# Two copies out of PSUM in an induced attention, moved to ScalarE in a planned kernel

## The chip, the cores and the metric

The kernel runs on one core of a Trainium2 chip. The metric is device time in microseconds (us), of one launch; the runs of the kernel before are 1744.55, 1745.02 and 1746.68 us, so their median is 1745.02.

## The reference

The input `x` is 4 batches of 12480 tokens with 128 channels. An induced attention with 32 learned points comes first, then a feed-forward layer with a squared relu, for every token:

```
scale = 1.0 / np.sqrt(C)
def mab(q, kv):
    s = scale * (q @ kv.transpose(0, 2, 1))
    s = s - s.max(-1, keepdims=True)
    a = np.exp(s)
    a /= a.sum(-1, keepdims=True) + 1e-09
    return a @ kv
h = mab(I, x)              # 32 rows a batch: the first attention
y = mab(x, h)              # every token on the 32 rows: the second attention
h = np.maximum(y @ w_in, 0.0)      # 128 -> 2048
out = h * h @ w_out                # 2048 -> 128
```

## The kernel before, in words

The tokens of a batch are cut into 13 units of 960; there are 52 units, and a unit has two halves of 480 tokens. Three kinds of work run side by side.

*The first attention* (class `First`) of a unit takes scores (`na` with `indT`, L430), a running maximum (`mx`, `neg`), an exponential (`e`), a transpose (`ep`, copied to `et`) and a product (`nb`) that is added to `hacc` and `zs`. It runs 14 units ahead of the feed-forward layer, so the last 13 or so units of the program have none of it. After the 13 units of a batch `first_end` joins the four partial results and makes `hT` and the matrix `hw`, which is `hT` times `w_in`; this is the change of batch, and the next batch's second attention starts from it.

*The second attention* (class `Second`) of a unit is done while the unit before it is in the feed-forward layer. Its scores `na` (L626) are 128 by 240 numbers in PSUM. `evict` copies them to SBUF as `ss` (L639, through the helper `copy`, so the profile has it at L235); `turn` transposes them on TensorE to `s2t`; `top` and `sub` (VectorE) take the maximum (`mx2`) and the difference `d`; `power` (ScalarE) is the exponential; `total`, `safe`, `invert` and `share` (VectorE) are the sum `z2`, its reciprocal `rz2` and the weights in `d`; `high` and `low` split them into `sk`; `back` turns them on TensorE into `ap`, 128 by 480 in PSUM; `stacked` copies `ap` to `sw` (L696, also L235 in the profile); `spread` sends `sw` with four DMAs on SP to `st`, the tile that the feed-forward layer of the next unit reads.

*The feed-forward layer* (`ffn_block`) does a half in four chunks (`quad`). A chunk has four matmuls `h` of 480 columns on `st` and `hw` into two double-bank PSUM tiles (there are two in all), two relus on ScalarE into `g` (L790), one square in place (L801), then on VectorE the rounded part `hi` (L805) and the rest `lo` (L809), and on TensorE 12 matmuls `op` (L822): `hi` with `wo_hi`, `hi` with `wo_lo`, `lo` with `wo_hi`. After the four chunks VectorE transposes `op` into `rows` (L837) and SP stores them.

The order of all this is not written out: every step is a task with an engine, a cost, a due time and what it needs, and the class `Plan` lays the tasks on the engines before anything is issued. Of the tasks that can start, an engine takes the one that is due first. A task for `"ACT|DVE"` goes to the engine where the plan lets it start first. Each engine then works through its instructions in that order, and an instruction that waits holds up all behind it.

Of the kernel before, what the change touches and what calls it, by code (L numbers as in the profile page):

```python
# [24 lines left out]
BLK = UNIT // 2  # L25
# [19 lines left out]
class Plan:  # L45
# [15 lines left out]
    def add(self, engine, ns, fn, due, needs=(), port=False, mode=None, takes=(), reads=(), late=None):  # L61

        if late is None:
            late = self.LATE["PE" if engine == "PE" else "other"] if due > self.begin else 0.0
        needs = [n for n in needs if n is not None]
        t = Task(engine.split("|"), ns, fn, due, needs, port, mode, takes, late, len(self.tasks))  # L70
        for b in list(takes) + list(reads):
            b.users.append(t)
        self.tasks.append(t)
        return t
# [80 lines left out]
def induced_attention_then_squared_relu_ffn(  # L155
# [8 lines left out]
    nc = tc.nc  # L164
# [10 lines left out]
    PERIOD, START, T_MAIN, NARROW, STEP = 32000.0, 2600.0, 66000.0, 6000.0, 1700.0  # L175
    W_DUE = [8000.0 + 6500.0 * k for k in range(8)]

    ST = "ACT|DVE"
    LATE_G1, LATE_OT = 150.0, 400.0


# [12 lines left out]
    def bank(name):  # L194
        return ps_m.tile([P, 512], F32, tag="m", name=name)
# [35 lines left out]
    add = plan.add  # L231
    ENG = {"ACT": nc.scalar.copy, "DVE": nc.vector.tensor_copy}

    def copy(task, dst, src):
        ENG[task.by](dst, src)  # L235
# [381 lines left out]
    class Second:  # L617
# [14 lines left out]
        def weigh(self, scored, where, bank_, due, step):  # L632
            v = {}
            n, s, u = self.n, self.s, self.u
            G = 2 * Q

            def evict():
                v["ss"] = att.tile([P, 2 * TS], F32, tag="ss", name=f"ss_{n}")
                copy(te, v["ss"], where())  # L639

            def turn():
                v["tp"] = tp = bank(f"s2t_{n}")
                for k in range(2):
                    nc.tensor.transpose(
                        tp[:TS, k * P:(k + 1) * P], v["ss"][:, k * TS:(k + 1) * TS], ident
                    )

            def top():
                v["tv"] = v["tp"][:TS, :2 * P].rearrange("t (g m) -> t g m", m=M)
                v["mx"] = tiny.tile([TS, G, 1], F32, tag="mx2", name=f"mx2_{n}")  # L650
                nc.vector.tensor_reduce(v["mx"], v["tv"], axis=AX.X, op=ALU.max)

            def sub():
                v["d"] = att.tile([TS, G, M], F32, tag="d", name=f"d_{n}")
                nc.vector.tensor_sub(v["d"], v["tv"], v["mx"].broadcast_to([TS, G, M]))

            def power():
                nc.scalar.activation(v["d"], v["d"], AF.Exp, scale=scale)

            def total():  # L660
                v["z"] = tiny.tile([TS, G, 1], F32, tag="z2", name=f"z2_{n}")
                nc.vector.tensor_reduce(v["z"], v["d"], axis=AX.X, op=ALU.add)

            def safe():
                nc.vector.tensor_scalar_add(v["z"], v["z"], 1e-9)

            def invert():
                v["rz"] = tiny.tile([TS, G, 1], F32, tag="rz2", name=f"rz2_{n}")
                nc.vector.reciprocal(v["rz"], v["z"])

            def share():
                nc.vector.tensor_mul(v["d"], v["d"], v["rz"].broadcast_to([TS, G, M]))  # L672

            def high():
                v["sk"] = att.tile([TS, Q, 2, 2, M], F32R, tag="sk", name=f"sk_{n}")
                nc.vector.tensor_copy(v["sk"][:, :, :, 0, :], v["d"].rearrange("t (k q) m -> t q k m", q=Q))

            def low():
                sk = v["sk"]
                nc.vector.tensor_sub(  # L680
                    sk[:, :, :, 1, :], v["d"].rearrange("t (k q) m -> t q k m", q=Q), sk[:, :, :, 0, :]
                )

            def back():
                v["ap"] = ap = bank(f"ap_{n}")
                for q in range(Q):
                    nc.tensor.matmul(  # L687
                        ap[:, q * TS:(q + 1) * TS],
                        v["sk"][:, q].rearrange("t k a m -> t (k a m)"),
                        identr[:TS, :TS], start=(q == 0), stop=(q == Q - 1), skip_group_check=True,  # L690
                    )

            def stacked():

                v["sw"] = att.tile([P, BLK], F32R, tag="sw", name=f"sw_{n}")
                copy(ts, v["sw"], v["ap"][:, :BLK])  # L696

            def spread():
                st = att.tile([P, 2, BLK], F32R, tag="st", name=f"st_{n}")
                for k in range(2):  # L700
                    for j in range(2):
                        nc.sync.dma_start(
                            st[j * 64:(j + 1) * 64, k, :].bitcast(F32),
                            v["sw"][k * 64:(k + 1) * 64, :].bitcast(F32),
                        )
                s["st", u] = st

            bt, ba, bw = Buffer("m"), Buffer("m"), Buffer("sw")
            self.bst = Buffer("st")
            d = due  # L710
            te = add("DVE", 317, evict, d, [scored], reads=[bank_])
            t = add("PE", 150, turn, d + step, [te], takes=[bt])
            t = add("DVE", 340, top, d + step, [t], reads=[bt])
            td = add("DVE", 340, sub, d + step, [t], reads=[bt])
            tp = add("ACT", 307, power, d + 2 * step, [td])
            t = add("DVE", 330, total, d + 3 * step, [tp])
            t = add("DVE", 70, safe, d + 3 * step, [t])
            t = add("DVE", 115, invert, d + 3 * step, [t])
            t = add("DVE", 340, share, d + 4 * step, [t], port=True)
            th = add("DVE", 210, high, d + 4 * step, [t], port=True)  # L720
            tl = add("DVE", 335, low, d + 5 * step, [th], port=True)
            t = add("PE", 460, back, d + 5 * step, [tl], takes=[ba])
            ts = add(ST, (455, 565), stacked, d + 6 * step, [t], takes=[bw], reads=[ba])
            self.ready = add("SP", 1000, spread, d + 7 * step, [ts], takes=[self.bst], reads=[bw])

    def narrow(second, f, g, due, step, begun=None):
# [193 lines left out]
```

## Time and profile before

| | us |
|---|---|
| runs of the kernel | 1744.55, 1745.02, 1746.68 |
| the profiled execution | 1748.76 |
| its span, first to last instruction | 1746.8 |
| TensorE busy (matmuls) | 1687.7 |
| VectorE busy | 1665.2 |
| ScalarE busy | 1588.2 |

In the lines of the profile PE is TensorE, PEld its weight loads, DVE VectorE, ACT ScalarE, SPq the DMA queue of SP. A line of a timeline has the start in us from the span's beginning, the length, the engine, the line of the kernel, the operation, what it writes and reads, how many are merged in it, and in brackets how long its engine sat idle before it and what ended that. A group has a count, the busy time in us, the mean length in ns, and the idle time before it. In the stretches each pair is busy time and number of instructions, in the order TensorE, weight loads, VectorE, ScalarE, GpSimd, then the granted clock, the share of the DMA engines and GB/s. Tile numbers are left out, so `mx` stands for the maxima of both attentions and `d` for all that is done in that tile.

The first 130 us or so are the loading of the weights and the first batch's first attention; then units follow each other in 32 us, and from about 1340 us on, where no first attention is left, in 29 to 31 us.

### The profile page before, as it was taken

To read this page: it belongs to the slowest core of one execution; us is meant where nothing else is said; L and a number is where in the kernel's file an instruction comes from. 1 tells how busy PE (TensorE), PEld (TensorE's weight loads), DVE (VectorE), ACT (ScalarE), POOL (GpSimd) and SP (SyncE) were. 2 spreads that over 40 slices of the span, in tenths; PEclk is the share of its full clock that TensorE was granted. 3 is DMA by queue.
4 is the path that set the end of the run, shared out by engine and by line. 5 is a ranking of instruction groups with operands and counts; after the bars stand their busy time and mean duration, and the time that the engine had idled before them with its cause. 6 is when DMAs were issued, how large, how long until landed. Compare 5 with 4: busy or idle time off the path is not lost.

```text
span 1746.8 us, 23651 instructions
## 1 busy us (share of the span) xinstructions
PE 1687.7 (97%) x8897; PEld 1339.3 (77%) x8897; DVE 1665.2 (95%) x1777; ACT 1588.2 (91%) x1581; POOL 25.8 (1%) x22
## 2 busy tenths in 40 slices
PE   7699999999999999999999999999999999999998
PEld 4378777777877777777777877777787888888886
DVE  5689999999999999999999999999999999999998
ACT  5399999999989999999998999999998999999997
POOL 1200000000000000000000000000000000000000
PEclk9699999999999999999999999999999999999999
DMA  9742342333333333333423333423211121211111
GB/s 207 128 68 47 63 74 53 62 68 63 61 59 57 60 66 63 63 57 63 73 47 63 64 56 63 74 47 62 40 29 35 29 40 29 41 29 37 32 27 30
DMA packets 428781, 101.61 MB, mean 58 GB/s; under 512 B 362844, under 2 KB 428156, under 8 KB 428668
## 3 DMA queue, kind: packets, MB, share of 16 engines
q1 hardware_dynamic: 428668, 100.11, 31.7%
q8 instruction: 70, 1.15, 0.3%
q14 instruction: 43, 0.35, 0.1%
HBM read 48.94 MB, written 25.56 MB: 43 GB/s over the span
## 4 chain that ended last, share of the span: by engine, by line
PE 51%; DVE 30%; issue 11%; ACT 6%; DMA 2%; SPq 0%; DVEq 0%; POOL 0%; ACTq 0%
PE op L822 35%; PE h L782 12%; DVE lo L809 10%; DVE hi L805 10%; ACT g L801 3%; ACT g L790 2%; DVE rows L837 2%; DVE xt L401 1%; PE na L626 1%; DMA xn<-in_x_dram 1%; DVE sw L235 1%; DVE d L672 1%; DVE sk L680 1%; PE wp L586 1%; DMA words_o<-in_moe_w_out_dram 1%
## 5 line engine op out<-in xcount | busy, mean ns | idle before, releaser
L809 DVE TENSOR_TENSOR lo<-g,hi 128x1920 fp32r<-128x1920 f32 x416 | 896.0, 2154 | 16.2 <-PE na L430 0.5
L790 ACT ACTIVATE g<-h 128x960 f32<-128x960 f32 x832 | 783.0, 967 | 96.1 <-PE h L782 82.6
L801 ACT ACTIVATE g<-g 128x1920 f32<-128x1920 f32 x416 | 752.9, 1810 | 8.2
L782 PE MATMUL h<-st,hw 128*128 128x480 f32 x1664 | 517.9, 389 | 12.7 <-ACT g L790 8.2
L805 DVE CAST hi<-g 128x1920 fp32r<-128x1920 f32 x416 | 477.6, 1148 | 25.1 <-ACT g L801 19.7
L822 PE MATMUL op<-lo,wo_hi 128*128 128x480 f32 x1664 | 459.3, 390 | 15.2 <-DVE lo L809 15.1
L822 PE MATMUL op<-hi,wo_hi 128*128 128x480 f32 x1664 | 462.6, 386 | 1.3 <-DVE hi L805 1.0
L822 PE MATMUL op<-hi,wo_lo 128*128 128x480 f32 x1664 | 432.3, 382 | 0.0
L782 PEld LDWEIGHTS h<-st,hw 128*128 128x128 f32 x1664 | 308.7, 189 | 104.3 <-ACT g L790 54.3
L822 PEld LDWEIGHTS op<-lo,wo_hi 128*128 128x128 f32 x1664 | 297.4, 189 | 87.5 <-DVE lo L809 42.0
L822 PEld LDWEIGHTS op<-hi,wo_hi 128*128 128x128 f32 x1664 | 304.1, 188 | 68.7 <-DVE hi L805 20.2
L822 PEld LDWEIGHTS op<-hi,wo_lo 128*128 128x128 f32 x1664 | 313.8, 189 | 49.9
L837 DVE STREAM_TRANSPOSE rows<-op 128x480 f32<-128x480 f32 x104 | 70.4, 677 | 1.3 <-PE op L822 1.2
L401 DVE STREAM_TRANSPOSE xt<-xq 128x960 f32<-128x960 f32 x39 | 45.7, 1172 | 4.3 <-PE na L626 4.3
L687 PEld LDWEIGHTS ap<-identr,sk 120*128 120x128 f32 x208 | 31.4, 193 | 7.3 <-issue 4.0
L626 PE MATMUL na<-xt,hT 128*32 128x240 f32 x416 | 32.7, 387 | 0.0
L687 PE MATMUL ap<-identr,sk 120*128 120x120 f32 x208 | 29.5, 265 | 2.5 <-DVE sk L680 2.5
L235 ACT COPY xt<-xtp 128x480 f32<-128x480 f32 x26 | 14.3, 559 | 16.4 <-PE xtp L415 16.4
L564 POOL TENSOR_SCALAR sums<-ones,zs 128x128 f32<-128x128 f32 x4 | 8.8, 2209 | 1228.1 <-PE lp L548 800.0
L464 PE MATMUL ep<-ident,e 128*120 128x128 f32 x104 | 21.5, 290 | 5.0 <-ACT e L456 3.3
L415 PE MATMUL xtp<-ident,xn 120*128 120x120 f32 x104 | 18.6, 319 | 7.6 <-DMA xn<-in_x_dram 7.6
L430 PE MATMUL na<-xt,indT 128*32 128x240 f32 x312 | 23.8, 378 | 0.9 <-DVE xt L401 0.9
(90 smaller groups left out, 616.6 us busy)
## 6 DMA issues: line engine op xcount, KB each, us to landing
xn<-in_x_dram SPq DMA_DIRECT2D x52, 480.0 KB, 4.9
st<-sw SPq DMA_DIRECT2D x208, 120.0 KB, 2.3
out_dram<-rows SPq DMA_DIRECT2D x416, 60.0 KB, 2.0
xq<-in_x_dram SPq DMA_DIRECT2D x156, 120.0 KB, 3.6
words_i<-in_moe_w_in_dram SPq DMA_DIRECT2D x4, 512.0 KB, 10.2
words_o<-in_moe_w_out_dram SPq DMA_DIRECT2D x4, 512.0 KB, 9.2
ind_sb<-in_inducing_dram SPq DMA_DIRECT2D x1, 16.0 KB, 1.6
```

The source lines that it names most:

```text
L235: ENG[task.by](dst, src)
L401: nc.vector.transpose(self.xt, v["xq"].rearrange("p g c -> p (g c)"))
L430: nc.tensor.matmul(where[q * M:(q + 1) * M, :], indT, self.xt[:, q * 2 * TS:(q + 1) * 2 * TS], start=True, stop=True,)
L626: nc.tensor.matmul(where[q * M:(q + 1) * M, :].rearrange("m (k t) -> m k t", k=2), self.s["hT"][:, :M], self.s["xt"][self.u].rearrange("c ...
L687: nc.tensor.matmul(ap[:, q * TS:(q + 1) * TS], v["sk"][:, q].rearrange("t k a m -> t (k a m)"), identr[:TS, :TS], start=(q == 0), stop=(q ...
L782: nc.tensor.matmul(c["hp"][:, l, :BLK], s["hw"][:, f * P:(f + 1) * P], s["st", u][:, k, :], start=True, stop=True,)
L790: nc.scalar.activation(v["g"][:, 2 * i:2 * i + 2, :], c["hp"][:, :, :BLK], AF.Relu)
L801: nc.scalar.activation(v["g"], v["g"], AF.Square)
L805: nc.vector.tensor_copy(v["hi"], v["g"])
L809: nc.vector.tensor_sub(v["lo"], v["g"], v["hi"])
L822: nc.tensor.matmul(w["op"][:, :BLK], wo[:, 4 * j + l, :], v[name][:, l, :], start=(j == m == l == 0), stop=(j == NQ - 1 and m == 2 and l = ...
L837: nc.vector.transpose(w["rows"].rearrange("p g c -> p (g c)"), w["op"][:, :BLK])
```

## The change

Both copies are made by ScalarE in all units. Before, `ss` was always VectorE's, and `sw` went to the engine that the plan chose: VectorE for 34 units, ScalarE for 18. The costs that the plan reckons with are 300 for `ss` (it was 317 on VectorE) and 437 for `sw` (it was 455 on ScalarE, 565 on VectorE).

```diff
-    ST = "ACT|DVE"
...
             def evict():
                 v["ss"] = att.tile([P, 2 * TS], F32, tag="ss", name=f"ss_{n}")
-                copy(te, v["ss"], where())
+                nc.scalar.copy(v["ss"], where())
...
                 v["sw"] = att.tile([P, BLK], F32R, tag="sw", name=f"sw_{n}")
-                copy(ts, v["sw"], v["ap"][:, :BLK])
+                nc.scalar.copy(v["sw"], v["ap"][:, :BLK])
...
-            te = add("DVE", 317, evict, d, [scored], reads=[bank_])
+            te = add("ACT", 300, evict, d, [scored], reads=[bank_])
...
-            ts = add(ST, (455, 565), stacked, d + 6 * step, [t], takes=[bw], reads=[ba])
+            ts = add("ACT", 437, stacked, d + 6 * step, [t], takes=[bw], reads=[ba])
```

Since the plan is made anew, the order changes on every engine, also among instructions that the diff does not name. Three places matter here. In the names, `hi_1_5_1_2` is the rounded part of batch 1, unit 5, half 1, chunk 2; `h_1_6_0_0` is the first pair of `h` of the next unit; the last number is a count.

VectorE in the second half of unit 5 of batch 1, before:

```order
L680 TENSOR_TENSOR sk_1_6_6562<-d_1_6_6492,sk_1_6_6562 120x8x32
L837 STREAM_TRANSPOSE rows_1_5_0_6583<-op_1_5_0_6411 128x480
L805 CAST hi_1_5_1_1_6593<-g_1_5_1_1_6547 128x1920
L235 CAST sw_1_6_6605<-ap_1_6_6588 128x480
L809 TENSOR_TENSOR lo_1_5_1_1_6611<-g_1_5_1_1_6547,hi_1_5_1_1_6593 128x1920
L805 CAST hi_1_5_1_2_6628<-g_1_5_1_2_6577 128x1920
```

And now:

```order
L675 CAST sk_1_6_6579<-d_1_6_6492 120x8x32
L836 STREAM_TRANSPOSE rows_1_5_0_6582<-op_1_5_0_6411 128x480
L679 TENSOR_TENSOR sk_1_6_6579<-d_1_6_6492,sk_1_6_6579 120x8x32
L804 CAST hi_1_5_1_1_6594<-g_1_5_1_1_6545 128x1920
L808 TENSOR_TENSOR lo_1_5_1_1_6607<-g_1_5_1_1_6545,hi_1_5_1_1_6594 128x1920
L804 CAST hi_1_5_1_2_6627<-g_1_5_1_2_6575 128x1920
```

The `sw` between `hi` and `lo` is gone from VectorE, and both parts of `sk` stand around `rows`.

TensorE at the border from unit 5 to unit 6 of batch 1, before:

```order
L822 MATMUL op_1_5_1_6570<-lo_1_5_1_1_6611,wo_hi_110 128x480 x4
L822 MATMUL op_1_5_1_6570<-hi_1_5_1_2_6628,wo_hi_110 128x480 x4
L782 MATMUL h_1_6_0_0_6641<-st_1_6_6615,hw_1_4611 128x480 x2
L822 MATMUL op_1_5_1_6570<-hi_1_5_1_2_6628,wo_lo_111 128x480 x4
L782 MATMUL h_1_6_0_1_6652<-st_1_6_6615,hw_1_4611 128x480 x2
```

And now:

```order
L821 MATMUL op_1_5_1_6566<-lo_1_5_1_1_6607,wo_hi_110 128x480 x4
L821 MATMUL op_1_5_1_6566<-hi_1_5_1_2_6627,wo_hi_110 128x480 x4
L821 MATMUL op_1_5_1_6566<-hi_1_5_1_2_6627,wo_lo_111 128x480 x4
L781 MATMUL h_1_6_0_0_6645<-st_1_6_6622,hw_1_4608 128x480 x2
L781 MATMUL h_1_6_0_1_6650<-st_1_6_6622,hw_1_4608 128x480 x2
```

All eight matmuls on `hi` of chunk 2 stand ahead of the new unit's first `h`; before, four of them did. At every second border of the middle it is six.

ScalarE at the start of a unit without a first attention (unit 6 of batch 3), before:

```order
L790 ACTIVATE g_3_6_0_0_14178<-h_3_6_0_1_14182 128x960
L801 ACTIVATE g_3_6_0_0_14178<-g_3_6_0_0_14178 128x1920
L790 ACTIVATE g_3_6_0_1_14204<-h_3_6_0_2_14192 128x960
L790 ACTIVATE g_3_6_0_1_14204<-h_3_6_0_3_14206 128x960
L801 ACTIVATE g_3_6_0_1_14204<-g_3_6_0_1_14204 128x1920
L790 ACTIVATE g_3_6_0_2_14239<-h_3_6_0_4_14232 128x960
L790 ACTIVATE g_3_6_0_2_14239<-h_3_6_0_5_14247 128x960
L658 ACTIVATE d_3_7_14250<-d_3_7_14250 120x256
```

And now:

```order
L789 ACTIVATE g_3_6_0_0_14180<-h_3_6_0_1_14178 128x960
L638 COPY ss_3_7_14199<-na_3_7_14183 128x240
L800 ACTIVATE g_3_6_0_0_14180<-g_3_6_0_0_14180 128x1920
L789 ACTIVATE g_3_6_0_1_14211<-h_3_6_0_2_14202 128x960
L789 ACTIVATE g_3_6_0_1_14211<-h_3_6_0_3_14213 128x960
L800 ACTIVATE g_3_6_0_1_14211<-g_3_6_0_1_14211 128x1920
L789 ACTIVATE g_3_6_0_2_14243<-h_3_6_0_4_14228 128x960
L789 ACTIVATE g_3_6_0_2_14243<-h_3_6_0_5_14245 128x960
L657 ACTIVATE d_3_7_14252<-d_3_7_14252 120x256
```

`ss` has come in between a relu and its square. Between the square and the exponential stand two relus, before and now; in every second unit the old order had one of them ahead of the square. On VectorE the sum `z2` stood behind the second `lo` of the unit where two relus came between, and ahead of it in the others; now it stands ahead of it in all.

## The prediction

> **What bounds the kernel now.** I read the busy time by stretches first, then VectorE's timeline through one unit, then the chain of waits in the same stretch. Columns of the first: length, then busy time of TensorE, its weight loads, VectorE and ScalarE, the granted clock, DMA.
>
> ```profile
> 300.00:500.00 200.00, 196.69 (x1041) 156.43 (x1040) 196.85 (x213) 186.24 (x183) 3.12 (x1) 1.00 0.34 61
> ...
> 1500.00:1700.00 200.00, 198.94 (x948) 163.50 (x947) 195.34 (x183) 193.78 (x175) 0.00 (x0) 1.00 0.17 32
> ```
>
> Three engines are nearly full in both regimes. In the long middle VectorE has 3.15 us idle in 200, ScalarE 13.8; in the last stretch, where no first attention is left, ScalarE has 6.2. So work taken from VectorE and given to ScalarE is worth what VectorE's own row of work and the waits between the engines leave of it. VectorE's timeline, one unit from its first `hi` to the next unit's (start, duration):
>
> ```profile
> 606.30 1.16 DVE L805 CAST hi<-g 128x1920 fp32r<-128x1920 f32 x1 [0.21 <-ACT g L801]
> ...
> 609.96 0.40 DVE L235 COPY ss<-na 128x240 f32<-128x240 f32 x1
> 610.27 0.15 DVE L449 SCALAR_TENSOR_TENSOR neg<-mx,neg 128x1 f32<-128x1 f32 x1
> ...
> 627.70 1.12 DVE L805 CAST hi<-g 128x1920 fp32r<-128x1920 f32 x1
> ...
> 629.30 2.14 DVE L809 TENSOR_TENSOR lo<-g,hi 128x1920 fp32r<-128x1920 f32 x1
> 631.36 1.15 DVE L805 CAST hi<-g 128x1920 fp32r<-128x1920 f32 x1
> 632.62 2.16 DVE L809 TENSOR_TENSOR lo<-g,hi 128x1920 fp32r<-128x1920 f32 x1
> 634.70 1.15 DVE L805 CAST hi<-g 128x1920 fp32r<-128x1920 f32 x1
> ...
> 638.33 1.16 DVE L805 CAST hi<-g 128x1920 fp32r<-128x1920 f32 x1 [0.22 <-ACT g L801]
> ```
>
> The unit takes 638.33 - 606.30 = 32.03 us. A `hi` and `lo` take 634.70 - 631.36 = 3.34, so two pairs 6.68; but 631.36 to 638.33 is 6.97. VectorE thus waits 0.29 once a unit, at the unit's first `hi`, and 31.74 is its own. What it waits for is the end of the chain (start, length, work):
>
> ```profile
> 610.68 0.59 DVE rows L837
> ...
> 613.53 0.31 DVE mx L651
> ...
> 615.90 0.33 DVE d L655
> 616.24 1.07 DVE hi L805
> ...
> 629.38 2.07 DVE lo L809
> 631.50 2.21 PE op L822 x8
> 633.71 0.44 PE h L782 x2
> 634.14 0.86 PE op L822 x4
> 635.01 0.45 PE h L782 x2
> 635.48 0.98 ACT g L790
> 636.49 1.82 ACT g L801
> 638.33 1.17 DVE hi L805
> ```
>
> Up to 631 the chain is mostly VectorE (a few of its steps stand at the top); then it leaves for TensorE (products of the old unit, the first two `h` of the new one) and ScalarE (relu, square) and comes back to the new unit's first `hi`.
>
> **The change, part by part.** The groups of the copies (count, busy us, mean ns):
>
> ```profile
> L235 DVE CAST sw<-ap 128x480 fp32r<-128x480 f32 x34 | 22.1, 650 | 0.0
> ...
> L235 DVE COPY ss<-na 128x240 f32<-128x240 f32 x52 | 20.8, 400 | 1.7 <-PE na L626 1.5
> ...
> L235 ACT COPY et<-ep 120x256 f32<-120x256 f32 x52 | 19.4, 374 | 3.7 <-PE ep L464 3.5
> ...
> L235 ACT CAST sw<-ap 128x480 fp32r<-128x480 f32 x18 | 9.9, 548 | 0.9 <-PE ap L687 0.9
> ```
>
> *Copies on ScalarE.* 52 `ss` and 34 `sw` go over; 18 `sw` were there already. `ss` never ran on ScalarE in this trace: its price lies between nothing, where ScalarE would have idled, and the 0.374 of `et`, which is a little longer; `sw` has its own row, 0.548. Together at most 0.92 us a unit, against 13.8 x 32.03/200 = 2.2 us idle in the middle and 6.2 x 29.9/200 = 0.9 in the tail. I take them as hidden in the middle. If that cover is gone, they cost what they last.
> [...]
>
> *VectorE's own time, middle.* `ss` costs the step 610.27 - 609.96 = 0.31. `sw` stands between a `hi` and its `lo`: 629.30 - 627.70 = 1.60 with it, 632.62 - 631.36 = 1.26 without, so only 0.34 comes back, not 0.65. That is 0.65 a unit. The new order also moves `z2` and `sk` in every second unit out of such a gap, where up to 0.2 is free; I take 0.2 off for those, 0.55 on average. VectorE's own way would be about 31.2.
>
> *The wait at the unit's border, middle.* The order shows that TensorE now does eight (every second unit: six) of the old unit's matmuls on its last-but-one `hi` before the first `h` of the new unit, where it did four.
>
> ```profile
> 628.87 0.73 PEld L822 LDWEIGHTS op<-hi,wo_hi 128*128 128x128 f32 x4
> ...
> 630.49 0.19 PEld L782 LDWEIGHTS h<-st,hw 128*128 128x128 f32 x1
> ...
> 633.33 0.40 PEld L782 LDWEIGHTS h<-st,hw 128*128 128x128 f32 x2
> ...
> 634.18 0.97 ACT L790 ACTIVATE g<-h 128x960 f32<-128x960 f32 x1 [0.25 <-PE h L782]
> ...
> 638.21 1.81 ACT L790 ACTIVATE g<-h 128x960 f32<-128x960 f32 x2
> ```
>
> From that `hi` (631.36) its matmuls start 1.21 later (in the chain: 631.50 + half of the eight, 632.57); eight take 630.49 - 628.87 = 1.62; a relu starts 634.18 - 633.33 = 0.85 after its `h`; two relus in a row are 1.81 - 0.97 = 0.84 apart; square follows relu by 636.49 - 635.48 = 1.01, and `hi` follows square by 638.33 - 636.49 = 1.84. With eight ahead: 1.21 + 1.62 + 0.85 + 0.84 + 1.01 + 1.84 = 7.37, a wait of 0.69. With six ahead the second `h` decides, 0.43 after the eight: 1.21 + 1.62 + 0.43 + 0.85 + 1.01 + 1.84 = 6.96, a wait of 0.28 as now. Mean 0.49, 0.20 more than now. Going through both kinds of unit step by step with these durations, TensorE also comes some 0.1 late to that `hi`, because it waits for `h` buffers that relu frees behind the two copies. So 0.25 of the 0.55 is lost: 0.30 a unit is left. Its ends are 0.55 (no added wait) and 0 (0.55 of it). Of the 34 units with both copies on VectorE five lie at a change of batch; 29 x 0.30 = 8.7 us, ends 16 and 0.
> `sw` also feeds the spread, four DMAs on SP, and the first `h` waits for them. On ScalarE `sw` stands behind a square (1.82) and no longer behind a `hi`, and on SP the spread no longer finds the four output stores of the half before ahead of it; the new order asks for `st` four matmuls, 0.86, later. I count nothing; if `st` is late all the same, by up to 1.82 - 0.86 = 0.96, the middle gains nothing and the border rival below holds.
>
> *The change of batch, three times.* There ScalarE starves and the chain runs through `sw`:
>
> ```profile
> 499.01 1.79 ACT L801 ACTIVATE g<-g 128x1920 f32<-128x1920 f32 x1
> ...
> 501.63 0.66 DVE L235 CAST sw<-ap 128x480 fp32r<-128x480 f32 x1
> ...
> 506.77 1.84 ACT L790 ACTIVATE g<-h 128x960 f32<-128x960 f32 x2 [3.26 <-PE h L782]
> ```
>
> On ScalarE `sw` follows this square and ends at 499.01 + 1.79 + 0.55 = 501.35 instead of 502.29: 0.9 earlier, while ScalarE waits 3.26 for the `h` that needs it. Three times 1.0 is 3 us, ends 0 and 5.
>
> *The last 12 units.* Here only `ss` moves. VectorE's first `hi` two units apart, then two small jobs of TensorE:
>
> ```profile
> 1443.10 1.16 DVE L805 CAST hi<-g 128x1920 fp32r<-128x1920 f32 x1
> ...
> 1502.94 1.15 DVE L805 CAST hi<-g 128x1920 fp32r<-128x1920 f32 x1
> ```
>
> ```profile
> 1436.87 0.16 PEld L626 LDWEIGHTS na<-xt,hT 128*32 128x32 f32 x8 [0.34 <-issue]
> ...
> 1437.41 0.30 PEld L782 LDWEIGHTS h<-st,hw 128*128 128x128 f32 x2 [0.39 <-issue]
> ...
> 1441.19 0.36 PEld L644 LDWEIGHTS s2t<-ident,ss 128*120 128x120 f32 x2
> ```
>
> Two units take 59.84, 29.92 each. VectorE saves between nothing (an `ss` that stood in the free time between a `hi` and its `lo`) and 0.31 a unit; I take 0.15. Its waits now come to less than 4.66 x 29.92/200 = 0.70 a unit, since the 0.11 between a `hi` and its `lo` (632.62 - 631.36 - 1.15) is in that idle time; I take 0.35. But the exponential now stands behind both relus of a chunk on ScalarE in every unit, and `z2`, which reads it, stands on VectorE ahead of the second `lo`, with all of VectorE's work queued behind it; the old order had the one or the other in a unit, not both. The chain from the third-last `lo` of the old unit to that `z2`: matmuls on a `lo` start 631.50 - 629.30 = 2.20 after it; the order has 46 matmuls of 480 columns from there to the `h` of the second relu, 46 x 0.86/4 = 9.9; `na` takes 0.54 + 0.34 = 0.88 of TensorE's time, `s2t` 0.36; the relu starts 0.85 after its `h`, the exponential 0.84 after the relu, and lasts some 0.4 (as `et` of its size). Sum 15.4. VectorE's own way between the same points is 2.07 for that `lo`, three pairs 10.02, and `mx2`, `rows`, `d` and a `hi`, 0.31 + 0.59 + 0.33 + 1.07: 14.4. So it waits 1.0 a unit where it waited 0.35: 0.5 lost with the 0.15 counted. Matmuls that come earlier than I reckon would shorten it, so I take 0.45: 12 x 0.45 = +5.4 us. The ends are -1.8 (no wait added, 0.15 saved) and +8 (0.65 lost).
>
> *The opening* has one `ss` to move and its `sw` is on ScalarE already: taken as nothing, ends -0.4 and +0.4, the length of one copy.
>
> Sum: -8.7 - 3 + 5.4 = -6.3 us on the profiled execution, 1748.76 us (span 1746.8): 1742.5. That execution lies 3.7 above the median of the runs, 1745.02; on that scale 1738.7. A measurement of this kernel can tell 0.2%, 3.5 us, from no change.
>
> **The rivals.**
> *VectorE's time comes back whole.* If TensorE reaches the border earlier than I reckon and no wait grows, the middle gives 16, the batch changes 5, the middle gives 16, the batch changes 5, the tail 1.8: 1745 - 23 = 1722. For it speaks VectorE's 98% and a chain that is mostly VectorE; against it the four extra matmuls ahead of `h`. Chance 0.18.
> [...]
> *The border eats it all.* The wait grows by 0.55 and the tail loses its 5.4: -3 + 5.4 = +2, 1747. Chance 0.22.
> *ScalarE becomes the bound (slower).* The copies stand ahead of relus that free the PSUM buffers for the next `h`. If ScalarE's idle time does not lie where they land, a middle unit takes 0.92 more on ScalarE while VectorE's 0.55 is lost in waits: +0.37 x 29 = 10.7, and with the tail's 8 and nothing at the batch changes 1745 + 19 = 1764. It decides from the point where less than 0.92 of ScalarE's 2.2 us idle time lies behind the copies, before the next square is due. Against it: the idle time is spread over waits for `h` all through the unit. Chance 0.08.
> That the change doesn't move the copies is excluded: the order shows all 104 on ScalarE.
>
> **How the numbers follow.** My case has 0.52. Its own time is 1738.7, taken as 1739, and its terms together spread by some 6 us: I put 0.38 of it below 1741.5 (0.2% under the median), 0.12 within 0.2% and 0.02 above. The border case is 0.02 faster, 0.16 within 0.2% and 0.04 slower, the full return faster, the ScalarE case slower. Faster 0.38 + 0.02 + 0.18 = 0.58; same 0.12 + 0.16 = 0.28; slower 0.02 + 0.04 + 0.08 = 0.14. The range goes from a little above the full return, 1725, to the border case with a worse tail, 1749; it leaves out half of the full return and the ScalarE case.
>
> **What would show it.** Right: `ss` near 0.36 and `sw` 0.55 on ScalarE; middle units alternating about 31.6 and 31.9; VectorE's wait at a unit's first `hi` near 0.3 and 0.7; tail units all alike near 30.4, with VectorE idle ahead of `z2`; the batch changes about 1 us shorter. Wrong: middle units of 31.3 or less, or of 32.0 and more; a tail below 29.9; ScalarE with no idle time left.

## The result, and the profile after

| | before | after |
|---|---|---|
| median of 4 runs, us | 1745.42 (1744.55 to 1746.68) | 1733.72 (1732.35 to 1735.98) |
| ratio | | 0.9934, 95% interval 0.9916 to 0.9951 |
| the profiled execution, us | 1748.76 | 1732.54 |

The change makes the kernel 11.7 us faster; 6.3 had been forecast. The two profiled executions differ by 16.2, since the one of before lies 3.3 above its median and the one of after 1.2 below.

First the two groups of the copies in the changed kernel (count, busy us, mean ns, idle time before them):

```profile
L695 ACT CAST sw<-ap 128x480 fp32r<-128x480 f32 x52 | 28.9, 556 | 4.0 <-PE ap L686 3.9
L638 ACT COPY ss<-na 128x240 f32<-128x240 f32 x52 | 18.7, 360 | 5.5 <-DVE mx L442 4.8 <-PE na L625 0.4 <-PE na L429 0.2
```

All 104 are on ScalarE, at 0.36 and 0.56 us. The same two stretches as before the change:

```profile
300.00:500.00 200.00, 198.34 (x1049) 158.23 (x1048) 195.05 (x201) 189.18 (x195) 3.19 (x1) 1.00 0.34 63
1500.00:1700.00 200.00, 197.14 (x939) 161.26 (x939) 192.07 (x170) 195.29 (x180) 0.00 (x0) 1.00 0.19 35
```

VectorE was busy for 196.85 and 195.34 of 200, now for 195.05 and 192.07; ScalarE went from 186.24 and 193.78 to 189.18 and 195.29. VectorE waits more, although the kernel is faster. Where it waits is in its timeline; these are the first `hi` of four successive units of the middle:

```profile
629.98 1.16 DVE L804 CAST hi<-g 128x1920 fp32r<-128x1920 f32 x1 [0.65 <-ACT g L800]
...
661.55 1.16 DVE L804 CAST hi<-g 128x1920 fp32r<-128x1920 f32 x1 [0.21 <-ACT g L800]
...
693.39 1.16 DVE L804 CAST hi<-g 128x1920 fp32r<-128x1920 f32 x1 [0.65 <-ACT g L800]
...
724.71 1.16 DVE L804 CAST hi<-g 128x1920 fp32r<-128x1920 f32 x1 [0.22 <-ACT g L800]
```

A unit's length is the distance between two such rows: 31.84 with the wait of 0.65 at its end, 31.32 with that of 0.22. VectorE's own time is what is left, 31.19 and 31.10. From here on the wait is always the one in the brackets. In the kernel before that is 0.22, and its own time 32.03 - 0.22 = 31.81; the prediction's 0.29 and 31.74 came from the pace of `hi` and `lo`, by which each of these waits comes out about 0.07 longer. (One unit has a further wait: 629.98 to 661.55 is 31.57.) In the last 12 units VectorE waits twice, at the first `hi` and for the exponential, ahead of `z2`:

```profile
1514.16 1.16 DVE L804 CAST hi<-g 128x1920 fp32r<-128x1920 f32 x1 [0.26 <-ACT g L800]
...
1520.22 0.42 DVE L661 TENSOR_REDUCE z<-d 120x8 f32<-120x256 f32 x1 [0.33 <-ACT d L657]
```

From the first `hi` of every unit follow the lengths by part; the experiments below are read by the same table. "Middle" is the mean of 27 units (2 to 10, 15 to 23, 28 to 36, counted from 0), "joins" the sum of the ten around the changes of batch (11 to 14, 24 to 27, 37, 38), "tail" the mean of the last 12 distances (39 to 50).

| kernel | middle | joins | tail |
|---|---|---|---|
| before | 32.03 | 334.9 | 29.93 |
| after | 31.57 | 330.9 | 30.17 |

27 x 0.455 = 12.3 and 3.9 are gained, 12 x 0.24 = 2.9 lost; units 0 and 1 give 0.4. That is 13.7 of the 16.2. The first unit also started 2.1 earlier (at 87.98 instead of 90.11; so the opening lasts some 90 us, not the 130 given further up). In two experiments that open just as the changed kernel does it started at 89.02 and 89.76, so most of this is scatter of the opening.

### The profile page after: what moved, and what is told of

It reads as the page before. It is cut to its first block, busy times and chain, and to the rows that moved or that the text cites. A ratio compares the mean times of both kernels' runs of the same rounds, so it can differ in the third digit from the quotient of the medians.

```text
span 1730.8 us, 23735 instructions
## 1 busy us (share of the span) xinstructions
PE 1676.5 (97%) x8897; PEld 1334.2 (77%) x8897; DVE 1636.3 (95%) x1691; ACT 1607.2 (93%) x1667; POOL 24.9 (1%) x22
## 4 chain that ended last, share of the span: by engine, by line
DVE 36%; PE 30%; issue 15%; ACT 14%; DMA 1%; DVEq 0%; SPq 0%; ACTq 0%
PE op L821 21%; DVE lo L808 14%; DVE hi L804 13%; ACT g L789 8%; PE h L781 7%; ACT g L800 6%; DVE xt L400 2%; DVE rows L836 2%; DVE z L661 1%; DVE mx L650 1%; DVE sk L679 1%; DVE d L654 1%; DVE mx L442 1%; PE na L625 1%; DVE d L671 0%
## 5 line engine op out<-in xcount | busy, mean ns | idle before, releaser
L781 PE MATMUL h<-st,hw 128*128 128x480 f32 x1664 | 513.4, 388 | 13.4 <-ACT g L789 6.4
L695 ACT CAST sw<-ap 128x480 fp32r<-128x480 f32 x52 | 28.9, 556 | 4.0 <-PE ap L686 3.9
L234 ACT COPY xt<-xtp 128x480 f32<-128x480 f32 x26 | 14.4, 557 | 14.5 <-PE xtp L414 14.2
L585 PE MATMUL wp<-w_in_sb,hT 128*128 128x512 f32 x32 | 20.0, 733 | 6.7 <-DVE hw L594 4.7
L661 DVE TENSOR_REDUCE z<-d 120x8 f32<-120x256 f32 x52 | 21.6, 415 | 3.8 <-ACT d L657 3.8
```

The source lines that it names most:

```text
L695: nc.scalar.copy(v["sw"], v["ap"][:, :BLK])
L781: nc.tensor.matmul(c["hp"][:, l, :BLK], s["hw"][:, f * P:(f + 1) * P], s["st", u][:, k, :], start=True, stop=True,)
```

## The experiments

All are timed against the kernel before on the same chip (its medians there: 1744.77, 1746.07, 1746.05 and 1745.69), and every ratio is to that. Edits are shown against the changed kernel, unless the text says against the kernel before. Where an instruction is moved, the plan's list of tasks is taken as it is and that task is put elsewhere in it; the loop over the units and the conditions are left out there ("...").

**Either half of the change.** With only `sw` always on ScalarE:

```diff
-            te = add("ACT", 300, evict, d, [scored], reads=[bank_])
+            te = add("DVE", 317, evict, d, [scored], reads=[bank_])
-                nc.scalar.copy(v["ss"], where())
+                nc.vector.tensor_copy(v["ss"], where())
```

> One half of the change: the weights ahead of their spreading (sw) always on ScalarE, the scores (ss) left on VectorE. My theory (VectorE's own time shrinks, part of it is lost in waits at the unit's border and in the tail): sw gives 0.34 a unit of the long middle, a little of it lost in waits, 29 x 0.25 = 7; the changes of batch give 3; the last 12 units have sw on ScalarE before too and give nothing. Near 1735, 10 under before. Rival (what counts is the order that the planner happens to make, not which copy moves): the time has no relation to this sum.

1731.39, ratio 0.9923 (0.9911 to 0.9936). With only `ss` there, `sw` back on either engine (in 44 of 52 cases the plan then takes VectorE):

```diff
-            ts = add("ACT", 437, stacked, d + 6 * step, [t], takes=[bw], reads=[ba])
+            ts = add("ACT|DVE", (455, 565), stacked, d + 6 * step, [t], takes=[bw], reads=[ba])
-                nc.scalar.copy(v["sw"], v["ap"][:, :BLK])
+                copy(ts, v["sw"], v["ap"][:, :BLK])
```

> The other half: ss always on ScalarE, sw on either engine by the planner as before. My theory: ss gives 0.31 a unit in the middle with no wait added there (the first h of a unit stands behind only two matmuls on the last-but-one hi), 29 x 0.3 = 9; nothing at the changes of batch; the tail loses 0.2 x 12 = 2.4 through the exponential. Near 1739, 6 under before. If the halves add up, the two gains sum to more than the 11.7 of the whole change, since neither half has the longer wait at the border. Rival (order alone): no relation.

1736.04, ratio 0.9952 (0.9939 to 0.9964). The `sw` half alone is at least as good as the whole change, and the two gains, 13.4 and 8.7, sum to 22. That the sum is more than 11.7 was expected, but the parts are not those expected:

| kernel | middle | joins | tail |
|---|---|---|---|
| `sw` alone | 31.67 | 327.9 | 30.19 |
| `ss` alone | 31.85 | 329.2 | 29.92 |

`sw` gave 9.8 in the middle where 7 was expected and 7.0 at the joins for 3, and lost 3.1 in the tail, where nothing was expected. `ss` gave 4.8 in the middle for 9, 5.7 at the joins for nothing (at two of the three changes of batch that plan has `sw` on ScalarE too), and did not lose the 2.4 in the tail. The errors partly cancel in the sums. And the first half shows something that no sum of copies explains, in the first `hi` of three units of the first batch:

```profile
312.54 1.15 DVE L804 CAST hi<-g 128x1920 fp32r<-128x1920 f32 x1
...
343.57 1.15 DVE L804 CAST hi<-g 128x1920 fp32r<-128x1920 f32 x1
...
374.59 1.15 DVE L804 CAST hi<-g 128x1920 fp32r<-128x1920 f32 x1
```

These units last 31.02 with no wait; in the second and third batch of the same kernel they last 31.95. The copies are the same. The plan is not: in the first batch TensorE does a unit's first `h` ahead of all matmuls on the old unit's last-but-one `hi`, in the others behind eight, and the second attention comes earlier in the unit (`sw` ends 16.7 us after the first `hi`, in the others some 24.0).

**Order and engine, all four pairs.** The plan of before, with both copies issued to ScalarE at the places that this plan gave them:

```diff
-            te = add("ACT", 300, evict, d, [scored], reads=[bank_])
+            te = add("DVE", 317, evict, d, [scored], reads=[bank_])
-            ts = add("ACT", 437, stacked, d + 6 * step, [t], takes=[bw], reads=[ba])
+            ts = add("ACT|DVE", (455, 565), stacked, d + 6 * step, [t], takes=[bw], reads=[ba])
```

> The plan of before, place for place, with both copies issued to ScalarE at the places where the plan had them. TensorE's order is that of before, with four matmuls of the last-but-one hi ahead of a unit's first h. My theory: without the longer wait at the border VectorE's 0.65 comes back almost whole, 29 x 0.6 = 17; the changes of batch give 3, the tail 1: near 1725, faster than the change itself. Rival (ScalarE is the bound, copies at places that were not planned for it delay its relus): no faster than the change, 1734 or more.

1743.97, ratio 0.9994 (0.9985 to 1.0003): no gain. My theory fell here. ScalarE's row and then the chain of waits show why (start, length, work):

```profile
623.69 1.81 ACT L800 ACTIVATE g<-g 128x1920 f32<-128x1920 f32 x1
625.41 0.54 ACT L695 CAST sw<-ap 128x480 fp32r<-128x480 f32 x1
```

```profile
625.43 0.53 ACT sw L695
625.96 0.02 issue
625.98 0.47 SPq L701
626.45 0.04 issue
626.49 2.34 DMA st<-sw
628.84 0.14 issue
628.97 0.68 PE h L781 x2
```

`sw` stands behind a square on ScalarE and ends at 625.96. The old unit's last-but-one `hi` starts 0.45 later in this kernel:

```profile
626.41 1.16 DVE L804 CAST hi<-g 128x1920 fp32r<-128x1920 f32 x1
```

In the kernel before, VectorE's `sw` ended at 628.73 + 0.65 = 629.38, 1.98 ahead of that `hi` (631.36):

```profile
628.73 0.65 DVE L235 CAST sw<-ap 128x480 fp32r<-128x480 f32 x1
```

From the end of `sw` to the first `h` that reads its spread there were about 4.2 us before; now there are 3.0, TensorE waits for the spread, and VectorE waits at the end of the chain. First TensorE's row, then two of VectorE's:

```profile
628.97 0.68 PE L781 MATMUL h<-st,hw 128*128 128x480 f32 x2 [0.20 <-DMA st<-sw]
```

```profile
633.83 1.16 DVE L804 CAST hi<-g 128x1920 fp32r<-128x1920 f32 x1 [0.67 <-ACT g L800]
...
665.83 1.16 DVE L804 CAST hi<-g 128x1920 fp32r<-128x1920 f32 x1 [0.65 <-ACT g L800]
```

A unit is 32.00: VectorE's own time fell by 0.48, to 31.33, and the wait rose by 0.45, to 0.67. The test of that reading takes this kernel and moves the square behind `sw` in 28 units, and nothing else:

```diff
+    def behind(t, other):
+        order.remove(t)
+        order.insert(order.index(other) + 1, t)
...
+        t, sq = marks["stacked", new], marks["square", old + "_1", 2]
...
+            behind(sq, t)
```

> The plan of before with both copies on ScalarE, as in the run that kept the old order, with one thing moved on ScalarE in 28 units: sw stands ahead of the square that it stood behind, 1.7 us earlier. Theory formed from that run (sw behind a square lets the spread land 0.2 to 0.4 after the first h of the unit asks for it, and the whole unit then waits for this loop through the second attention): no h waits for st, the wait of 0.67 at the first hi falls to 0.28, the middle 0.35 a unit shorter, 10 less, near 1734. Rival (copies on ScalarE cost their own length at places that were not planned for them, wherever they stand): 1744, or later, since the square is 0.45 later.

1731.52, ratio 0.9915 (0.9902 to 0.9929): 14.5 under the kernel before, where the same order without the swap was 0.8 under it. `sw` now ends 1.8 earlier in the unit (22.3 us after its first `hi`, 24.1 without the swap), no `h` waits for `st`, and the wait is back at its old size:

```profile
628.82 1.16 DVE L809 CAST hi<-g 128x1920 fp32r<-128x1920 f32 x1 [0.21 <-ACT g L805]
...
660.40 1.16 DVE L809 CAST hi<-g 128x1920 fp32r<-128x1920 f32 x1 [0.21 <-ACT g L805]
```

Not all of the 1.8 reaches the spread, which starts only 0.6 earlier, since on SP it now finds output stores ahead of it:

```profile
618.74 1.94 SPq L847 DMA_DIRECT2D out_dram<-rows  x4
...
620.78 2.40 SPq L702 DMA_DIRECT2D st<-sw  x4
```

It is enough. Units are 31.56 long, 31.34 of VectorE's own and 0.22 of wait, as long as those of the changed kernel (31.57). So the old order gives the middle's whole gain too, once `sw` stands ahead of that square.

The fourth pair: the plan of the changed kernel, with the 52 `ss` and the 34 `sw` that VectorE made before back on VectorE at this plan's places:

```diff
-                nc.scalar.copy(v["ss"], where())
+                nc.vector.tensor_copy(v["ss"], where())
-                nc.scalar.copy(v["sw"], v["ap"][:, :BLK])
+                own = n in ("0_0", "0_1", "0_2", "1_2", "2_2", "2_12") or (self.b == 3 and u)
+                (nc.scalar.copy if own else nc.vector.tensor_copy)(v["sw"], v["ap"][:, :BLK])
```

> The plan of the changed kernel, place for place, but every copy that VectorE made before (52 ss, 34 sw) issued to VectorE at the place where this plan has it. With the kernel before, the changed one and the old order with both copies on ScalarE this gives all four pairs of order and engine. My theory (both are needed): VectorE's own time in the middle goes up again by 0.5 to 0.65 and about half of it falls into the waits of the new order: units near 31.9, 1744 to 1748, no better than before. Rival A (the order alone makes the gain): 1734 to 1736. Rival B (the engine alone, the order being worth nothing): 1745, with units of 32.0 and the waits at the first hi as they were in the kernel before.

1759.86, ratio 1.0081 (1.0067 to 1.0095), slower than before and than any of the three theories had it:

```profile
610.05 1.16 DVE L805 CAST hi<-g 128x1920 fp32r<-128x1920 f32 x1 [0.21 <-ACT g L801]
...
642.88 1.16 DVE L805 CAST hi<-g 128x1920 fp32r<-128x1920 f32 x1 [0.84 <-ACT g L801]
```

The unit between is 32.83, the next is 31.98. The wait of 0.84 is longer than the 0.65 of the changed kernel. At these borders `sw` on VectorE ends so late (634.80 + 0.65 = 635.45) that the first `h`, at 638.47, follows it by the same 3.0 us as in the kernel with the old order, so the spread is likely the cause; that was not tested. All four, in us a unit of the middle (length; VectorE's own time and its wait at the first `hi`):

| | copies on VectorE | copies on ScalarE |
|---|---|---|
| order of before | 32.03 (31.80 + 0.23) | 32.00 (31.33 + 0.67) |
| order of after | 32.37 (31.87 + 0.50) | 31.57 (31.16 + 0.41) |

(All are means over the 27 units.) At these places the engine alone gives next to nothing, the order alone costs 0.34, both together give 0.46.

**The price of the border.** The kernel before, with the old unit's four further matmuls moved ahead of the first `h` of the new one at 27 borders (the edit is against the kernel before):

```diff
+        first = marks["h", new + "_0", 0, 0]
+        ops = [marks["op", old + "_1", 2, 1, i] for i in range(2)]
...
+            for t in ops:
+                order.remove(t)
+                order.insert(order.index(first), t)
```

> The kernel before with one thing moved on TensorE at 27 unit borders: eight of the old unit's matmuls on its last-but-one hi stand ahead of the first h of the new unit, where four did; the copies stay on VectorE. My theory (the order at the border has a price of its own): VectorE's wait at the first hi grows from 0.29 to 0.69, units 32.4 instead of 32.0, 27 x 0.4 = 11 more, near 1756. Rival (TensorE has room at the border, or the second h decides): no change, 1745.

1755.72, ratio 1.0057 (1.0045 to 1.007), and the wait grew as I had worked out, by 0.43 (0.22 to 0.65) for 0.40:

```profile
642.28 1.16 DVE L809 CAST hi<-g 128x1920 fp32r<-128x1920 f32 x1 [0.63 <-ACT g L805]
...
674.68 1.16 DVE L809 CAST hi<-g 128x1920 fp32r<-128x1920 f32 x1 [0.65 <-ACT g L805]
```

Units are 32.40. So the border costs that, on either engine. Then its reverse in the changed kernel, the first two pairs of `h` behind four matmuls in all 32 units:

```diff
+        last = marks["h", new + "_0", 1, 1]
+        late = [marks["op", old + "_1", 2, 1, i] for i in range(2)]
...
+            for t in reversed(late):
+                behind(t, last)
```

> The changed kernel with one thing moved on TensorE at 32 unit borders inside a batch: the first two pairs of h of the new unit stand behind four of the old unit's matmuls on its last-but-one hi instead of six or eight; the matmuls passed follow them. My theory (the wait at the first hi is what is left of VectorE's gain): the waits of 0.65 and 0.21 go, middle units 31.1 to 31.3 all alike, 29 x 0.4 = 12 less, near 1722. Rival (another loop sets the unit's length, such as the h buffers or the spread, whose transfer would land as late as these h now ask for it): 0 to 4 less, 1730 to 1734.

1736.15, ratio 0.9943 (0.9931 to 0.9956): no gain, the middle even 31.72. The wait of 0.65 is down to 0.33, but it stands at the head of a unit in which VectorE now waits four times:

```profile
630.69 1.16 DVE L808 CAST hi<-g 128x1920 fp32r<-128x1920 f32 x1 [0.33 <-ACT g L804]
...
637.92 0.42 DVE L651 TENSOR_REDUCE mx<-s2t 120x8 f32<-120x256 f32 x1 [0.30 <-PE s2t L644]
...
642.05 0.42 DVE L662 TENSOR_REDUCE z<-d 120x8 f32<-120x256 f32 x1 [0.24 <-ACT d L658]
...
646.13 2.16 DVE L812 TENSOR_TENSOR lo<-g,hi 128x1920 fp32r<-128x1920 f32 x1 [0.34 <-DVE rz L669]
```

TensorE's row at the border ahead of this unit shows that the rival named beforehand is what happened:

```profile
626.27 1.10 PE L782 MATMUL h<-st,hw 128*128 128x480 f32 x4 [0.32 <-DMA st<-sw]
```

`h` now asks for `st` earlier than the spread can land: `sw` ended at 623.26, and the `h` again follows it by 3.0 us. At about every second border of the middle it is so, and in the unit behind such a border the transposed scores `s2t` start 6.8 us after the first `hi` (6.0 in the changed kernel), and VectorE waits for them and for what follows from them. Those units last about 31.9, the others, where `h` did not wait for `st`, about 31.5. The expectation had named the spread and not worked out when it lands.

**The tail, and ScalarE.** The exponential put ahead of the second relu of its chunk in ten of the last 12 units:

```diff
+        if new in name[42:]:
+            t = marks["power", new]
+            order.remove(t)
+            order.insert(order.index(marks["relu", old + "_0", 5]), t)
```

> The changed kernel with one thing moved on ScalarE in ten of the last 12 units: the exponential of the second attention stands ahead of the second relu of its chunk instead of behind it. My theory (the exponential behind two relus makes z2 late, and VectorE waits 0.33 for it): VectorE no longer waits ahead of z2, 10 x 0.33 = 3.3 less, near 1730.5, tail units near 29.85. Rival (ScalarE, 195.3 of 200 busy there, sets the tail): the wait moves to the unit's first hi, no change.

1734.49, ratio 0.9931 (0.9917 to 0.9944), as the change. From the waits between 1400 and 1650 us (total, count, longest), of after and then of this kernel:

```profile
DVE z L661 <- ACT d L657: 3.0, 8, 0.4
DVE hi L804 <- ACT g L800: 1.8, 7, 0.3
```

```profile
DVE hi L809 <- ACT g L805: 3.3, 13, 0.3
```

The wait ahead of `z2` is gone. The one at a unit's first `hi` stayed, and a new one came two `hi` ahead of it, so that the tail is no shorter (30.28 for 30.17):

```profile
1508.99 1.16 DVE L809 CAST hi<-g 128x1920 fp32r<-128x1920 f32 x1 [0.27 <-ACT g L805]
...
1516.22 1.16 DVE L809 CAST hi<-g 128x1920 fp32r<-128x1920 f32 x1 [0.25 <-ACT g L805]
```

Both copies made twice, on ScalarE:

```diff
                 nc.scalar.copy(v["ss"], where())
+                nc.scalar.copy(v["ss"], where())
...
                 nc.scalar.copy(v["sw"], v["ap"][:, :BLK])
+                nc.scalar.copy(v["sw"], v["ap"][:, :BLK])
```

> The changed kernel with each of the two copies made twice in a row on ScalarE, all else in place: ScalarE gets 0.8 us a unit more (0.25 for ss, 0.55 for sw). My theory: mostly hidden in the middle, 0.1 to 0.3 a unit, and up to 0.5 in the tail, where ScalarE has little idle time: 5 to 15 in all, 1739 to 1749. Rival (ScalarE has become the bound): 0.8 x 52 = 42, near 1775.

1754.83, ratio 1.0056 (1.0043 to 1.007), 10.1 over the kernel before, so some 22 over the change: middle 32.01, tail 30.67. The 0.8 us that this was to put on ScalarE was an estimate. In the changed kernel ScalarE goes on 621.80 - 621.36 = 0.44 after the start of a `sw` and 631.79 - 631.55 = 0.24 after that of an `ss`, 0.68 together:

```profile
621.36 0.55 ACT L695 CAST sw<-ap 128x480 fp32r<-128x480 f32 x1
621.80 1.84 ACT L789 ACTIVATE g<-h 128x960 f32<-128x960 f32 x2
...
631.55 0.36 ACT L638 COPY ss<-na 128x240 f32<-128x240 f32 x1
631.79 1.83 ACT L800 ACTIVATE g<-g 128x1920 f32<-128x1920 f32 x1
```

For that a unit pays 0.44 in the middle and 0.50 in the tail, more than I expected and about two thirds and three quarters of what a full ScalarE would make of it.

**The scores earlier.** The fast units of the `sw` half had the second attention earlier in the unit. One number of the plan puts it there, in the changed kernel (to 3 and to 4 us) and in the kernel before (to 3):

```diff
-    PERIOD, START, T_MAIN, NARROW, STEP = 32000.0, 2600.0, 66000.0, 6000.0, 1700.0
+    PERIOD, START, T_MAIN, NARROW, STEP = 32000.0, 2600.0, 66000.0, 3000.0, 1700.0
```

> The changed kernel with one number of the plan changed: the step of TensorE that starts the second attention (the scores) is due 3 us after a unit's start instead of 6. In the new order the scores stand about one pair of hi and lo earlier in the unit, the transposition back (ap) ahead of the last matmuls on the first chunk's lo, and the first h of a unit ahead of all matmuls on the last-but-one hi. My theory as it stands (a loop through the second attention, the spread and the unit's first h sets the unit's length; VectorE's own time is some 31.1): VectorE no longer waits at the first hi, middle units near 31.0, 29 x 0.55 = 16 less than the change, near 1718. Rival (TensorE's or ScalarE's own time has become the bound at 31.5 to 31.6 whatever the order): the same as the change, 1734.

> The same with the scores due 4 us after the unit's start. The order differs from batch to batch; the first h of a unit stands ahead of all matmuls on the last-but-one hi in most units. My theory: units near 31.0 to 31.3 where it does, near 1721. Rival (another engine's own time): 1734.

> The kernel before, copies on VectorE, with the scores due 3 us after the unit's start instead of 6. My theory: VectorE's own 31.7 a unit is all that is left, 29 x 0.3 = 9 less than before, near 1736; the difference to the changed kernel with the same number then is the copies' own time, 18 or so. Rival (the gain of the change is one of order alone, and the copies' engine doesn't matter): as fast as the changed kernel with the same number.

| kernel | median, us | ratio to before | middle | joins | tail |
|---|---|---|---|---|---|
| after, 3 us | 1714.18 | 0.9813 (0.9798 to 0.9828) | 31.25 | 318.4 | 30.40 |
| after, 4 us | 1728.70 | 0.9896 (0.9881 to 0.9911) | 31.51 | 325.1 | 30.24 |
| before, 3 us | 1726.08 | 0.9883 (0.9867 to 0.99) | 31.57 | 323.7 | 30.35 |

The first beats both kernels of this study and the expected 1718, but again not by the parts: the middle gives 9 us for 16, and another 12.5 come from the joins, where nothing was expected. The second missed its 1721. In its first batch units are near the expected 31.2, in the next two they run in threes of about 31.4, 30.4 and 33.4. The third is 10 faster than its 1736; there too the joins give 11 that were not counted. In the first kernel the first `hi` rows of the middle have no wait, and VectorE is busy for 196.86 of 200 us, as in the kernel before:

```profile
600.00:800.00 200.00, 199.61 (x1071) 162.32 (x1070) 196.86 (x197) 195.37 (x199) 0.00 (x0) 1.00 0.37 63
```

```profile
621.52 1.16 DVE L804 CAST hi<-g 128x1920 fp32r<-128x1920 f32 x1
...
683.81 1.16 DVE L804 CAST hi<-g 128x1920 fp32r<-128x1920 f32 x1
```

These rows are two units apart. The two take 62.29, 31.15 each, and the mean of the middle is 31.25; VectorE's own time in the changed kernel was 31.16. So here little but its own time is left. Against the kernel before with the same number the change is worth 11.9; but that plan puts 49 of the 52 `sw` on ScalarE by itself, so these 11.9 are mostly `ss`, and the expectation's 18 was not a test of both copies.

## Why the prediction was right, and where its sizes were off

The kernel became faster, as forecast, and in the middle by the mechanism that was forecast: VectorE's own time shrinks, and part of that goes into a longer wait at the border. But 11.7 us were gained for 6.3, because the middle gave more and the tail lost less than reckoned; both errors point the same way.

- *What bounds the kernel.* Right as far as it went: VectorE's own time and a wait at the first `hi`. What closes little more than 1 us behind that chain (4.2 us where 3.0 are needed) is the spread of `sw`, which the prediction named and gave no time of its own. The run with the old order and the one with the reversed border both ran into it, each with `h` 3.0 us behind the end of `sw`.
- *VectorE's own time, middle.* Forecast 0.55 less, measured 0.64 less (31.80 to 31.16). The 0.2 taken off for `z2` and `sk` in every second unit is not seen, the two kinds of unit differ by 0.06. (The gap itself does have such room: in the kernel before a `lo` starts 624.69 - 623.42 = 1.27 after its `hi` with a `sk` of 0.29 between them, and 1.26 without.) The four pairs show that this gain is no property of the copies: on their old places they gave 0.47, on the new ones 0.71. The shorter units, of about 31.35, come close to the 31.3 that the prediction had listed as a sign of being wrong.
- *The wait at the border.* Forecast 0.28 and 0.69, measured 0.30 and 0.72 by the prediction's way of counting (0.22 and 0.65 in the brackets), and its cause is shown by the same move in the kernel before. (The chain's 631.50 and half of 2.21 make 632.6, not the prediction's 632.57; in the changed kernel the step is 1.21 all the same, 622.58 to 623.79.) With the 0.1 by which TensorE was to come late it was to cost 0.25 a unit; it cost 0.18. So the middle gained 0.46 a unit where 0.30 was forecast, 12.3 us for 8.7: own time accounts for 0.09 of the difference and the wait for 0.07.
- *The spread, counted at nothing.* In the changed kernel it holds: the plan moved `ap` and `sw` up, and the first `h` follows the end of `sw` by 3.7 us or more. The clause that `st` might be late all the same, and the middle then gains nothing, is what the old order with both copies on ScalarE does: 32.00 for 32.03.
- *The change of batch.* 3 forecast, 3.9 measured over ten units. ScalarE's wait for `h` there, 3.26 before, is shorter:

```profile
498.95 2.73 ACT L789 ACTIVATE g<-h 128x960 f32<-128x960 f32 x3 [1.76 <-PE h L781]
```

  At the first two changes the unit that holds this wait takes 37.01 before, 36.98 in the order of after with the copies on VectorE, 36.31 in the order of before with them on ScalarE, and 36.16 after. So there the engine of the copies is worth 0.7 to 0.8, near the 1.0 forecast; the rest of the 3.9 has no run of its own.
- *The tail.* This is the other term that was mis-sized: 2.9 lost for 5.4. A wait of 1.0 ahead of `z2` was forecast in place of 0.35 in all. It came at 0.33 to 0.41, with 0.25 at the first `hi`, so that VectorE's waits grew by 0.23 a unit and not by 0.65, and nothing was saved of its own time. The exponential's place is not the cause by itself, since taking that wait away gave nothing. Nor is the copy that moved: in the order of after the tail is 30.17 with `ss` on ScalarE and 30.18 with `ss` on VectorE, and `ss` alone on ScalarE, in its own order, leaves it at 29.92. (The order of before with `ss` on ScalarE has 30.04.) So most of the loss belongs to the order; which step of it stays open.
- *The rivals.* VectorE's time did not come back whole: 0.64 of own time gave 0.46. VectorE's 98% (196.85 of 200), which spoke for that rival, forecasts no gain by itself: in the run with the old order VectorE lost both copies, and the time was 1743.97 for 1744.77, until `sw` was put ahead of a square. ScalarE did not become the bound of the middle, but it is close: some 0.68 us more costs 0.44.
- *The sum.* -6.3 forecast; by the same terms -12.3 - 3.9 + 2.9 - 0.4 = -13.7 on the profiled execution, -11.7 between the medians.

## What to carry to other kernels

Where three engines are nearly full and the order comes from a plan, moving an operation to another engine changes two things, the engine's load and the order, and each has a price of its own: measure the four pairs, here 32.03, 32.00, 32.37 and 31.57. Read which chains end shortly behind the one that you relieve, above all a transfer fed by the operation that moves: its place in the new queue (here behind a square of 1.8 us) can take the whole gain, and one swap in that queue can give it back. When a move makes an instruction ask earlier for its data, work out first when the data can be there. And compare an expectation with the runs part by part: several sums here came near with parts that were off both ways.

## What the runs showed of the hardware that was not expected

- From the end of `sw` on ScalarE to the first `h` that reads its spread went 628.97 - 625.96 = 3.01 us: 0.47 on SP's queue and 2.34 for a transfer (the spread is four DMAs of 120 KB each). In the run with the reversed border it was 626.27 - 623.26 = 3.01 as well.
- A copy costs its engine by its place. `sw` on VectorE lasts 0.65, but takes 635.37 - 634.80 = 0.57 of VectorE's time where it stands between a `lo` and the next `hi`, as here in the order of after, and 0.34 between a `hi` and its `lo`, as the prediction has it for the kernel before.

```profile
634.80 0.65 DVE L696 CAST sw<-ap 128x480 fp32r<-128x480 f32 x1
635.37 1.15 DVE L805 CAST hi<-g 128x1920 fp32r<-128x1920 f32 x1
```
